# Attention prologue of a fused attention, MoE and ELU-FFN kernel: bias read-outs after the next hidden products, blocks loaded one step earlier, extra products of ones on TensorE

## The chip, the cores and the metric

One core of a Trainium2 chip runs the whole kernel. The metric is the device time of one execution in microseconds (us); the median of three runs of the kernel before is 1201.24 us (1200.07 to 1203.87). The engines are TensorE (PE; its weight loads are PEld), VectorE (DVE), ScalarE (ACT), GpSimd (POOL) and SyncE (SP), which issues the DMAs.

## The reference

Attention over 2 batches, 8 heads, 576 positions and head size 64, with a position bias that a small network makes; its output goes through an MoE and an ELU feed-forward layer. Only the attention is touched.

```python
scores = scale * np.matmul(q, k.transpose(0, 1, 3, 2))
psi_rel = np.log1p(np.abs(rel))                       # 576 x 576
psi_i = np.log1p(np.maximum(pos[:, None], 1.0))
x = (psi_rel / psi_i)[..., None]
h = np.maximum(x @ w1 + b1, 0.0)                      # 32 hidden values
bias = h @ w2                                         # 8 heads
scores = scores + bias.transpose(2, 0, 1)[None, :, :, :]
attn = softmax(scores)
out = np.matmul(attn, v)
```

## The kernel before

**Steps.** The 16 pairs of head pair and batch are "blocks". A step is one tile of up to 128 query rows of one block: scores on TensorE (`emit_qk`, letter Q, tile `sc`, 8 matmuls), bias added and the row minimum taken on DVE (R and S, tile `et`), exponentials on ACT (E and F), and one step later transposes (T, U, V), products with the values (a, tile `av`) and evacuation (X). The first four steps are the 64-row tile of blocks 0 to 3, so each of them needs a block of its own.

**Blocks.** `load_qk(i)` asks SP for block i in four DMAs of 288 KB, into slot i mod 3 of a ring; `prep(i)` splits it into high and low parts in six DVE operations (two casts, two for `qs`, two for `kl`), one per letter p of the prologue, three per p of the first steps. `LQ` and `PS` say at which step blocks 2 and 3 are loaded and at which step each `prep` is queued.

**Bias.** The bias is made in 36 groups of 16 rows, over the prologue and the first fourteen steps. A group has three stages. Letter H (`bias_hh`, `bias_h`): four hidden tiles `ht` of 304 to 576 columns, each put on ACT or DVE by `pick`, which adds up estimated loads of both engines. Letter P or M (`bias_p`, `bias_mm`): the products `bps` on TensorE, four column tiles of 32. Letter O (`bias_o`, `bias_out`): one or two read-outs `o` by ACT or DVE, again by `pick`, and a store to the scratch `scr` in HBM. A step's bias tile `bt` is loaded from `scr` (B, and L through `bias_loads`) once its groups are stored. At most two groups of `ht` may wait for their product (`len(hq) < 2`), and `ht` lies in two pairs of buffers: the tiles of group k take those of group k-2, which the product of group k-2 reads. From step 0 on the products of a group of up to 512 columns lie in one PSUM bank (`psC[1]`), so a product waits for the read-out of the product before it; a longer group takes a bank of `psB` as well.

**Order.** The order on every engine is the order in which these letters are emitted: `PRO` for the prologue, `ORD_S` for steps 0 to 2 (three groups a step), `ORD_A` while groups are left (two a step), `ORD_B` after. Each engine works through its own queue in that order, SP through its DMAs. In the prologue read-outs of the first groups go through `psA`, which the scores use later. Eight products of ones (`WARM`) open the kernel on TensorE while the first DMAs run.

After the bias is done a step holds scores, transposes and value products only; then come the MoE and the feed-forward layers, over 80% of the time.

Of the kernel before, what the change touches and what calls it, by code (L numbers as in the profile page):

```python
# [32 lines left out]
QB = [5, 4]  # L33
AB = 2
BD = 1
PRO = "HHPOH0PpOHpPOHPOkkBHppPkkppOQHmO"
LQ = [100, 101]
LS = [5, 9, 13, 21]
LV = [0, 1, 2, 3, 19, 20, 28, 32]
ACC = [2.6, 3.1]  # L40
WARM = 8
PS = [[1, 0], [2, 1], [3, 2], [4, 13], [5, 16], [6, 20], [7, 26]]
ORD_S = "RXTSMOHUapaMOHEaaNpFaLMOVQH"
ORD_A = "RXTSMOHUapaEaaNpFaLMOVQH"
ORD_B = "RTSNUXaafLEafaappFVQ"
TOFF = [0, 128, 256, 384, 512]
TROW = [128, 128, 128, 128, 64]
# [173 lines left out]
def attention_moe_elu_ffn_kernel(  # L221
# [14 lines left out]
    act, dve, pe, pool, sp = nc.scalar, nc.vector, nc.tensor, nc.gpsimd, nc.sync  # L236
# [12 lines left out]
    def psum(name, bufs, shape):  # L249
        p = ctx.enter_context(tc.tile_pool(name=name, bufs=bufs, space=bass.MemoryType.PSUM))  # L250
        return lambda nm: p.tile(shape, F32, tag=name, name=nm)
# [3 lines left out]
    psC = [psum("psC", 1, [128, 512]), psum("psD", 1, [128, 512])]  # L255
# [4 lines left out]
    ones = cp.tile([128, 128], F32, name="ones")  # L260
# [856 lines left out]
    def attention(fill):  # L1117
# [21 lines left out]
        def load_qk(i):  # L1139
            hp, b = blocks[i]  # L1140
            loaded[i] = []
            for src, rt in ((qt, ring[0]), (kt, ring[1])):
                r = rt[:, i % 3]
                for o in (0, 64):
                    sp.dma_start(out=r[o:o + 64], in_=src[b, hp])
                    yield
                loaded[i].append(r)

        def load_now(i):
            for _ in load_qk(i):  # L1150
                pass
# [7 lines left out]
        prep_q = []  # L1159
# [3 lines left out]
        def prep(i):  # L1163
            qs = qkp.tile([128, 2, S], F32R, tag="qs", name="qs")
            kh = qkp.tile([128, 2, S], F32R, tag="kh", name="kh")
            kl = klp.tile([128, 2, S], F32R, tag="kl", name="kl")
            prepped[blocks[i]] = qs, kh, kl
            qr, kr = loaded.pop(i)
            rem = dve if i < 4 else pool
            for dst, src in ((qs, qr), (kh, kr)):  # L1170
                dve.tensor_copy(dst, src)
                load["d"] += 0.73
                yield
            for h in range(2):
                o = slice(64 - 64 * h, 128 - 64 * h)
                rem.tensor_tensor(out=qs[o, h], in0=qr[o, h], in1=qs.bitcast(F32)[o, h], op=ALU.subtract)
                yield
            for h in range(2):
                rem.tensor_tensor(out=kl[:, h], in0=kr[:, h], in1=kh.bitcast(F32)[:, h], op=ALU.subtract)
                if rem is dve:  # L1180
                    load["d"] += 1.5
                yield
# [17 lines left out]
        def emit_qk(s):  # L1200
            hp, b, t = steps[s]
            qs, kh, kl = prepped[hp, b]
            r = TROW[t]
            etile[s] = (
                ep.tile([128, 2 * S], F32, tag="e", name="et"),
                tp.tile([128, 2], F32, tag="nmx", name="nmx"),
                tp.tile([128, 2], F32, tag="sm", name="sm"),
            )
            sc = [psA("sc") for _ in range(2)]
            qc = slice(TOFF[t], TOFF[t] + r)  # L1210
            for h in range(2):
                for w, last in ((kh, False), (kl, True)):
                    for x in range(2):
                        kc = slice(HALF * x, HALF * x + HALF)
                        pe.matmul(sc[h][0:r, x, 0:HALF], qs[:, h, qc], w[:, h, kc], start=not last, stop=last)  # L1215
            for h in range(2):
                scs[s, h] = sc[h]
# [40 lines left out]
        def emit_tr(s, h):  # L1258
            r = TROW[steps[s][2]]
            et = etile[s][0]  # L1260
            if h == 0:
                aT[s] = atp.tile([128, 9, 128], F32, tag="aT", name="aT")
            p = psB("tr")
            for j in range(4):
                c0 = 640 * h + 128 * j
                pe.transpose(p[:, 128 * j:128 * j + r], et[0:r, c0:c0 + 128], ident[0:r, 0:r])  # L1266
            src = p.rearrange("p (j q) -> p j q", j=4)[:, :, 0:r]
            dst = aT[s][:, 4 * h:4 * h + 4, 0:r]
            if h == 0:
                act.activation(out=dst, in_=src, func=ACTF.Copy)  # L1270
            else:
                dve.tensor_copy(dst, src)

        def emit_trl(s):
            r = TROW[steps[s][2]]
            et = etile.pop(s)[0]
            p = psB("trl")
            pe.transpose(p[:, 0:r], et[0:r, 512:640], ident[0:r, 0:r])  # L1278
            act.activation(out=aT[s][:, 8, 0:r], in_=p[:, 0:r], func=ACTF.Copy)
# [51 lines left out]
        def run_step(s):  # L1331
            d = s - LAG
            cur, tr = s < NS, 0 <= d < NS
            for x in ORD_S if s < 3 else ORD_A if no[0] < GRP else ORD_B:
                if x == "T" and tr:
                    emit_tr(d, 0)
                elif x == "U" and tr:
                    emit_tr(d, 1)
                elif x == "V" and tr:
                    emit_trl(d)  # L1340
                elif x == "Q" and s + 1 < NS:
                    emit_qk(s + 1)
                elif x in "RS" and cur:
                    emit_ttr(s, "RS".index(x))
                elif x in "EF" and cur:
                    emit_exp(s, "EF".index(x))
                elif x == "N" and 1 <= s <= NS:
                    emit_norm(s - 1)
                elif x == "X":
                    x_evac()  # L1350
                elif x == "a":
                    av(1)
                elif x == "M":
                    bias_p()
                elif x == "O":
                    bias_o()
                elif x == "H":
                    bias_hh()
                elif x == "p":
                    for _ in range(3 if s < 4 else 1):  # L1360
                        prep_next()
                    do_bg(1)
                elif x == "L":
                    bias_loads(s)
                elif x == "f":
                    fill_pe(s)
            if tr:
                av_q.extend(av_pieces(d))

        U = up.tile([128, S], F32, name="U")  # L1370
        bpsi = csb[:, C_PSI:C_PSI + NM]
        dve.memset(ones, 1.0)
        wp = psC[0]("warm")
        for _ in range(WARM):
            pe.matmul(wp[:, 0:128], ones, ones, start=True, stop=True)
        sp.dma_start(out=csb, in_=cst)
        sp.dma_start(out=U, in_=lext)
        load_now(0)
        dve.tensor_scalar(bpsi, bpsi, csb[:, C_B1:C_B1 + 1], None, ALU.mult)
        dve.tensor_scalar(U, U, csb[:, C_W1:C_W1 + 1], None, ALU.mult)  # L1380

# [8 lines left out]
        def bias_h(g):  # L1390
# [3 lines left out]
            for c in range(4):  # L1394
# [4 lines left out]
                if pick(0.187 + n / 1200, 0.129 + n / 1920) == "a":  # L1399
                    act.activation(out=h[:, 0:n], in_=U[:, 0:n], func=ACTF.Relu, bias=bpsi[:, m:m + 1])  # L1400
                else:
                    dve.tensor_scalar(h[:, 0:n], U[:, 0:n], bpsi[:, m:m + 1], 0.0, ALU.add, ALU.max)
                ht.append(h)
# [59 lines left out]
        def bias_hh():  # L1463
            if nh[0] < GRP and len(hq) < 2:
                bias_h(gorder[nh[0]])
                nh[0] += 1
# [13 lines left out]
                load_bias(nk[0])  # L1480
                nk[0] += 1

        ld = [load_qk(1)]
        for x in PRO:
            if x == "H":
                bias_hh()
            elif x == "P":
                bias_p(True)
            elif x == "m":
                bias_p()  # L1490
            elif x == "O":
                bias_o()
            elif x == "0":
                prep_q.append(prep(0))
            elif x == "p":
                prep_next()
            elif x == "k":
                next(ld[0], None)
            elif x == "B":
                load_bias(nk[0])  # L1500
                nk[0] += 1
            elif x == "Q":
                emit_qk(0)
        next(ld[0], None)
        for s in range(NS + LAG):
            if 100 + s in LQ:
                load_now(2 + LQ.index(100 + s))
            for i, s0 in enumerate(LS):
# [4 lines left out]
            if s in LV:  # L1513
                load_v(LV.index(s))
            for i, s0 in PS:
                if s == s0:
# [15 lines left out]
            if s == 15:  # L1532
                w = csb[:, C_WG:C_WG + 4 * E].rearrange("p (k e) -> p k e", k=4)
# [86 lines left out]
```

## Time and profile before

| | |
|---|---|
| median of 3 runs | 1201.24 us |
| profiled execution | 1202.67 us, span 1200.8 us |
| busy share PE, PEld, DVE, ACT, POOL | 97%, 83%, 76%, 53%, 6% |
| chain that ended last | PE 93%, ACT 2%, DVE 2%, DMA 1%, issue 1% |
| stretch of the span that the change touches | about the first 115 us |

The span runs from the first to the last instruction of the program. The profiled execution has 1.87 us around its span, and lies 1.43 us over the median. The busy shares are averages over stages with different limits, so the stage of the change is read by itself, in windows and in order of time.

### The profile page before, as it was taken

What the parts mean: (1) busy time and instruction counts of PE and PEld (TensorE: products, weight loads), DVE (VectorE), ACT (ScalarE), POOL (GpSimd) and SP (SyncE); (2) the same over time, 40 slices, a digit from 0 to 9 for tenths busy, and PEclk for the clock granted to TensorE, in tenths of its full rate; (3) what the DMA queues carried; (4) which work ended last, traced back from release to release, by engine and by line L of the source; (5) the groups of instructions that cost most, each with busy time, mean ns of one, the idle gap of its engine ahead of it and who ended that gap; (6) DMA issues with size and microseconds to landing.
All of it is one profiled execution on the core that took longest, in us unless ns stands there. A gap on an engine that the chain in (4) does not pass through costs nothing.

```text
span 1200.8 us, 19646 instructions
## 1 busy us (share of the span) xinstructions
PE 1167.2 (97%) x7432; PEld 996.8 (83%) x7432; DVE 910.5 (76%) x1936; ACT 632.7 (53%) x1428; POOL 67.9 (6%) x91
## 2 busy tenths in 40 slices
PE   6899999899999999999999999999999988999998
PEld 3466988788888888888888888888888876788887
DVE  6688888755687878778778788787776468788875
ACT  6898678554333344444443444444434346777763
POOL 0101643000000000000000000000000001000000
PEclk8999999999999999999999999999999999999999
DMA  7676641111112133333242323332311101111102
GB/s 207 212 227 213 184 141 48 36 53 53 36 36 97 62 106 89 104 90 94 74 132 64 104 90 104 99 96 78 115 45 53 53 3 35 53 53 36 36 1 79
DMA packets 36285, 104.78 MB, mean 87 GB/s; under 512 B 4064, under 2 KB 4192, under 8 KB 36192
## 3 DMA queue, kind: packets, MB, share of 16 engines
q1 hardware_dynamic: 36192, 103.54, 28.3%
q8 instruction: 58, 0.95, 0.3%
q14 instruction: 35, 0.29, 0.1%
HBM read 81.88 MB, written 21.64 MB: 86 GB/s over the span
## 4 chain that ended last, share of the span: by engine, by line
PE 93%; ACT 2%; DVE 2%; DMA 1%; issue 1%; POOL 0%; SPq 0%; DVEq 0%; ACTq 0%; POOLq 0%
PE y L724 41%; PE m L537 38%; PE sc L1215 3%; PE bps L1418 3%; PE av L1297 3%; PE tr L1266 3%; PE av L1307 1%; PE av L1294 1%; PE trl L1278 0%; PE lg L880 0%; ACT ht L1400 0%; DMA bt<-scr 0%; ACT et L1240 0%; ACT o L1450 0%; DVE c L569 0%
## 5 line engine op out<-in xcount | busy, mean ns | idle before, releaser
L537 PE MATMUL m<-oh,w1h 128*128 128x256 f32 (+1 forms) x1120 | 335.3, 299 | 3.9 <-DVE c L569 1.4
L537 PE MATMUL m<-oh,w1l 128*128 128x256 f32 (+1 forms) x1120 | 329.7, 294 | 3.8 <-ACT u L550 1.6
L537 PE MATMUL m<-ol,w1h 128*128 128x256 f32 (+1 forms) x1120 | 329.5, 294 | 2.8 <-DVE c L569 1.3
L724 PE MATMUL y<-w2h,hh 128*128 128x512 f32 x720 | 284.5, 395 | 2.9 <-ACT hh L644 1.5
L724 PE MATMUL y<-w2h,hl 128*128 128x512 f32 x720 | 283.4, 394 | 0.0
L724 PE MATMUL y<-w2l,hh 128*128 128x512 f32 x720 | 282.6, 392 | 0.8 <-DVE w2l L437 0.8
L537 PEld LDWEIGHTS m<-oh,w1h 128*128 128x128 f32 x1120 | 210.0, 188 | 47.4 <-ACT u L550 13.3
L537 PEld LDWEIGHTS m<-ol,w1h 128*128 128x128 f32 x1120 | 210.4, 188 | 22.6 <-DVE c L569 1.9
L537 PEld LDWEIGHTS m<-oh,w1l 128*128 128x128 f32 x1120 | 210.3, 188 | 5.6 <-ACT u L550 2.3
L724 PEld LDWEIGHTS y<-w2h,hh 128*128 128x128 f32 x720 | 135.1, 188 | 18.8 <-ACT hh L644 2.3
L724 PEld LDWEIGHTS y<-w2h,hl 128*128 128x128 f32 x720 | 135.1, 188 | 17.8
L550 ACT ACTIVATE p<-m 128x256 f32<-128x256 f32 (+1 forms) x160 | 65.8, 411 | 157.3 <-PE m L537 153.2
L724 PEld LDWEIGHTS y<-w2l,hh 128*128 128x128 f32 x720 | 135.2, 188 | 16.2 <-DVE w2l L437 1.4
L550 ACT ACTIVATE u<-m 128x256 f32<-128x256 f32 (+1 forms) x160 | 65.9, 412 | 131.8 <-PE m L537 128.5
L600 ACT ACTIVATE hh<-c 128x512 fp32r<-128x512 f32 (+3 forms) x128 | 72.1, 563 | 109.7 <-DVE c L569 109.6
L755 DVE SCALAR_TENSOR_TENSOR acc<-y,P,acc 128x512 f32<-128x512 f32 x126 | 94.5, 750 | 38.5 <-PE y L724 36.6
L603 DVE SCALAR_TENSOR_TENSOR hl<-c,hh 128x512 fp32r<-128x512 f32 (+3 forms) x128 | 77.5, 606 | 20.5 <-ACT hh L600 18.8
L569 DVE TENSOR_TENSOR c<-m,u 128x256 f32<-128x256 f32 (+1 forms) x80 | 36.7, 458 | 72.4 <-PE m L537 70.7
L1225 DVE CUSTOM_DVE_ANT_0 et<-sc,bt 128x576 f32<-128x576 f32 (+1 forms) x80 | 58.1, 751 | 16.0 <-PE sc L1215 14.2
L1240 ACT ACTIVATE et<-et,nmx 128x576 f32<-128x576 f32 (+1 forms) x80 | 61.3, 772 | 0.3 <-DVE nmx L1225 0.3
L430 ACT ACTIVATE w2h<-raw 128x512 fp32r<-128x512 f32 x80 | 48.6, 625 | 23.2 <-PE y L724 12.4
L1418 PE MATMUL bps<-ht,csb 128*32 128x512 f32 (+17 forms) x352 | 48.8, 520 | 9.9 <-ACT ht L1400 5.7
(138 smaller groups left out, 1566.7 us busy)
## 6 DMA issues: line engine op xcount, KB each, us to landing
raw<-w1p SPq DMA_DIRECT2D x32, 512.0 KB, 3.8
raw<-w2p SPq DMA_DIRECT2D x32, 512.0 KB, 3.6
scr<-o SPq DMA_DIRECT2D x36, 295.5 KB, 2.5
bt<-scr SPq DMA_DIRECT2D x16, 576.0 KB, 4.2
cw<-w1d SPq DMA_DIRECT2D x16, 512.0 KB, 4.4
wsc<-ca SPq DMA_DIRECT2D x32, 256.0 KB, 4.5
cw<-w2d SPq DMA_DIRECT2D x16, 512.0 KB, 4.5
raw<-wsc SPq DMA_DIRECT2D x16, 512.0 KB, 3.6
```

Of the source, the lines that this page charges most:

```text
L430: act.activation(out=dst(bh.get()), in_=src(), func=ACTF.Copy)
L537: lambda e, w=w, o=o, j=j, k=k: pe.matmul(x["ap"](bank), w.get()[:, ai, j, :], o.get()[:, bi, j, :], start=(k == 0 and i in (1, 2, 5)), st ...
L550: lambda e: act.activation(out=b.get()[:, 0:N], in_=x["ap"](bank), func=ACTF.Copy),
L569: lambda e: eng[e].tensor_tensor(out=blk(b.get()[:, half * N:half * N + N], rev), in0=ap(p), in1=ap(q), op=ALU.add),
L600: op([("A", cA(w))], lambda e: act.activation(out=hh(), in_=ap(), func=ACTF.Relu), r=sk, w=wh, after=gate_)
L603: lambda e: dve.scalar_tensor_tensor(out=bl.get()[:, d], in0=ap(), scalar=0.0, in1=hhf(), op0=ALU.max, op1=ALU.subtract),
L724: lambda e, a=a, w=w, f=f, i=i, y=y, c=c: pe.matmul(y.get(), a.get()[:, c], w.get(), start=(f == 0 and i == 0), stop=(f == 3 and i == 2)),
L755: lambda e: dve.scalar_tensor_tensor(out=a.get(), in0=y.get(), scalar=P[0][:, n, e_:e_ + 1], in1=a.get(), op0=ALU.mult, op1=ALU.add),
L1215: pe.matmul(sc[h][0:r, x, 0:HALF], qs[:, h, qc], w[:, h, kc], start=not last, stop=last)
L1225: dve.tensor_tensor_reduce(out=e.rearrange("p (x j) -> p x j", x=2), in0=sc[0:r, :, 0:HALF], in1=biast[hp, t][0:r, h].rearrange("p (x j) - ...
L1240: act.activation(out=e, in_=e, func=ACTF.Exp, scale=-1.0, bias=nmx[0:r, h:h + 1], accum_out=sm[0:r, h:h + 1])
L1418: pe.matmul(p[32 * c:32 * c + 32, d0 - lo:d1 - lo], csb[:, C_W2:C_W2 + 32], ht[c][:, d0:d1], start=True, stop=True, tile_position=(0, 32 * c),
```

## The change

The prologue makes seven groups instead of six, with nine instead of seven groups of hidden tiles begun, and two casts of block 1. Within a step each O moves behind the H that followed it (MOH becomes MHO; at the end of the step MOVQH becomes MHOVQ). Block 1 is loaded right behind block 0, block 2 in the place of block 1, block 3 at step 0 instead of step 1; `prep(1)` starts in the prologue, `prep(2)` and `prep(3)` a step earlier. The new letter w puts four products of ones on TensorE: three times in the prologue and twice in step 0.

```diff
-PRO = "HHPOH0PpOHpPOHPOkkBHppPkkppOQHmO"
-LQ = [100, 101]
+PRO = "HHPOH0PpOHpPOHPOkkBHppPwkkHppOQmHOwm1pHpOw"
+LQ = [0, 100]
-PS = [[1, 0], [2, 1], [3, 2], [4, 13], [5, 16], [6, 20], [7, 26]]
-ORD_S = "RXTSMOHUapaMOHEaaNpFaLMOVQH"
-ORD_A = "RXTSMOHUapaEaaNpFaLMOVQH"
+PS = [[2, 0], [3, 1], [4, 13], [5, 16], [6, 20], [7, 26]]
+ORD_S = "RXTSMHOwUapaMHOwEaaNpFaLMHOVQ"
+ORD_A = "RXTSMHOUapaEaaNpFaLMHOVQ"
...
+                elif x == "w" and s == 0:
+                    warm(4)
...
+        def warm(k):
+            wp = psC[0]("warm")
+            for _ in range(k):
+                pe.matmul(wp[:, 0:128], ones, ones, start=True, stop=True)
+
...
         load_now(0)
+        load_now(1)
...
-        ld = [load_qk(1)]
+        ld = [load_qk(2)]
...
-            elif x == "0":
-                prep_q.append(prep(0))
+            elif x in "01":
+                prep_q.append(prep(int(x)))
+            elif x == "w":
+                warm(4)
```

## Rows read from the trace of the kernel before

**Rows 1.** Windows: us, busy us (x instructions) of each engine, granted clock, DMA.

```profile
40.00:50.00 10.00, 9.09 (x60) 3.93 (x60) 7.97 (x17) 8.19 (x19) 1.49 (x1) 1.00 0.50 172
60.00:70.00 10.00, 10.00 (x107) 6.72 (x106) 9.24 (x32) 9.22 (x26) 0.81 (x2) 1.00 0.64 211
130.00:140.00 10.00, 10.00 (x105) 9.18 (x104) 8.90 (x25) 6.90 (x21) 5.46 (x7) 1.00 0.62 220
```

**Rows 2.** Chain that ended last, first 200 us: start, us, what.

```profile
17.68 4.60 DMA bt<-scr
...
24.45 2.65 PE bps L1418 x8
...
28.84 2.53 PE bps L1418 x8
31.37 2.11 PE sc L1215 x8
...
59.07 1.26 PE sc L1215 x8
...
108.16 1.06 PE sc L1215 x8
...
113.77 1.05 PE sc L1215 x8
...
117.31 1.07 PE sc L1215 x8
```

**Rows 3.** Windows of 2 us around the stretch at the lower clock, columns as Rows 1.

```profile
22.00:24.00 2.00, 0.00 (x0) 0.00 (x0) 1.70 (x6) 1.50 (x3) 0.00 (x0) 0.96 0.91 234
24.00:26.00 2.00, 1.55 (x7) 0.84 (x11) 2.00 (x5) 0.00 (x0) 0.00 (x0) 0.50 1.10 381
...
34.00:36.00 2.00, 2.00 (x13) 0.69 (x12) 1.42 (x5) 1.16 (x4) 0.00 (x0) 0.98 1.07 308
```

**Rows 4.** Waits, first 150 us: who for whom, us, times, longest.

```profile
ACT o L1450 <- PE bps L1418: 15.4, 19, 3.6
```

**Rows 5.** Waits, first 30 us.

```profile
ACT o L1450 <- PE bps L1418: 7.5, 5, 3.6
```

**Rows 6.** Timeline, one pair of products: start, us, engine, line, operation, shapes [idle before].

```profile
101.01 0.60 PE L1418 MATMUL bps<-ht,csb 128*32 128x464 f32 x4
...
101.42 0.57 PE L1418 MATMUL bps<-ht,csb 128*32 128x464 f32 x4
```

**Rows 7.** Timeline, 15 to 28 us.

```profile
15.29 1.54 DVE L1176 TENSOR_TENSOR qs<-ring,qs 64x576 fp32r<-64x576 f32 x2
...
16.22 2.66 ACT L1400 ACTIVATE ht<-U,csb 128x544 f32<-128x544 f32 x4
16.76 1.41 DVE L1179 TENSOR_TENSOR kl<-ring,kh 128x576 fp32r<-128x576 f32 x2
...
18.62 1.15 PE L1418 MATMUL bps<-ht,csb 128*32 128x512 f32 x16
...
23.82 1.29 DVE L1402 TENSOR_SCALAR ht<-U,csb 128x528 f32<-128x528 f32 x3
```

**Rows 8.** DMA issues, 1.6 to 4.2 us: count, KB each, median us to landing.

```profile
ring<-qt SPq DMA_DIRECT2D x2, 288.0 KB, 4.6
ring<-kt SPq DMA_DIRECT2D x2, 288.0 KB, 5.8
```

**Rows 9.** Timeline, first 6 us, TensorE.

```profile
1.05 3.78 PE L1375 MATMUL warm<-ones 128*128 128x128 f32 x16 [1.05 <-DVE ones L1372]
```

**Rows 10.** Timeline, 35 to 60 us, ACT and DVE.

```profile
35.84 0.91 ACT L1450 ACTIVATE o<-bps,csb 128x496 f32<-128x496 f32 x2 [0.84 <-PE bps L1418]
36.64 0.70 ACT L1400 ACTIVATE ht<-U,csb 128x480 f32<-128x480 f32 x1
38.46 0.91 ACT L1450 ACTIVATE o<-bps,csb 128x480 f32<-128x480 f32 x2 [1.12 <-PE bps L1418]
...
58.91 0.96 DVE L1452 TENSOR_SCALAR o<-bps,csb 128x384 f32<-128x384 f32 x2 [1.49 <-PE bps L1418]
```

More of the change, by code (lines that the diff above doesn't have):

```diff
@@ L1372, in attention @@
         dve.memset(ones, 1.0)
-        wp = psC[0]("warm")
-        for _ in range(WARM):
-            pe.matmul(wp[:, 0:128], ones, ones, start=True, stop=True)
+        warm(WARM)
         sp.dma_start(out=csb, in_=cst)
```

## The prediction, made before the change was run

> **What bounds the kernel now.** I read the windows first. Of 1200.8 us the change touches the first 115. From 60 to 110 us TensorE reads 10.00 busy in 10, but loads weights for only 6.72 of them, while from 130 us, with the bias done, it loads for 9.18 [rows 1]. So a busy TensorE is partly waiting in the bias stage, and ACT, at 9.22, is as near its limit. Before 60 us nothing is full: 9.09, 8.19 and 7.97 of 10 for TensorE, ACT and DVE.
>
> The chain of waits gives the milestones [rows 2]. Step 0's score pass waits for the bias tile (landed at 17.68 + 4.60 = 22.28 us). The scores of step 1 start at 31.37, of step 4 at 59.07, of step 13 at 108.16, of step 14 at 113.77, of step 15 at 117.31. So steps 4 to 12 last (108.16 - 59.07) / 9 = 5.45 us each, step 13, with one group, 5.61, and a step without bias 3.54. TensorE's granted clock is at the lower level (0.50, 1.2 GHz) from just before 24 to about 34 us, after a gap in which it ran nothing (22 to 24 us) [rows 3]; there two products take 2.65 and 2.53 us [rows 2] where a pair of 512 columns and a rest at the higher level takes 1.15 [rows 7].
>
> The wait which the change names is in the table of waits: ACT's read-outs wait 15.4 us in all for their products, 19 times [rows 4], 7.5 us of it before 30 us [rows 5].
>
> **Where the wait goes.** A product ends as one: four records start together, the other four 0.41 us later, all over by 101.99 [rows 6]. So all its `ht` buffers come free at its end, 0.98 us after its start. Before, ACT waits there with the read-out. In the new order the hidden tiles of group k+2 come first, and they take the very buffers which the product of group k reads; so H waits for the same end. Behind it, O stands later by H, and the next product waits for O, because both use one PSUM bank. A slot before, from read-out to read-out: read-out, hidden tile, tail of the product: 38.46 - 35.84 = 2.62 us, with one hidden tile of four on ACT [rows 10]. After, with the same split: hidden tile 0.6 (0.66 of [rows 7], for fewer columns), read-out 0.9, product 1.0, two hand-overs of 0.05 to 0.1 (the product of [rows 6] runs from 101.01 to 101.99): 2.6 to 2.7. The wait changes its owner; the loop keeps its length. Per slot I take nothing.
>
> **The change part by part**, against the profiled execution (1202.67 us, span 1200.8; 1.43 above the median).
>
> A, to the scores of step 1. Each start below is the end of the last input, from the durations of [rows 7], [rows 6] and [rows 10]: hidden tile 0.66 on ACT and 0.43 on DVE, read-out 0.9, product of 16 records 1.15, of 8 about 1.05, prep operation 0.72; engines as `pick` gives them by the code's own sums. Two hidden tiles of group g2 now stand on DVE ahead of the `kl` of block 0: its scores, and the product behind them, slip from 18.62 to 19.5. That product (g1) ends at 20.65; three tiles on ACT to 22.65; read-out to 23.55; product g2 to 24.8; two tiles to 26.1; read-out to 27.0; product g3 to 28.25; one tile and the read-out to 29.8 (DVE's three tiles beside them); product g4 to 30.95. On DVE three prep operations, a hidden tile and the read-out of g4 end at 33.2, so product g5 ends at 34.35. Then the scores of step 1: 34.35 against 31.37, **+3.0**, with one group more done. The clock's return is in it (products at 1.05 to 1.15). The wait for `bt` is covered: DVE comes to the score pass at 26.
>
> In A cost nothing: the products of ones. Unknown at the higher level; eight records take 1.9 us by the first eight products of the kernel (3.78 for 16) [rows 9], and no less than 0.9 if they run at twice that pace. TensorE's gaps of 3.0, 2.2, 1.6 and 2.3 us (20.65 to 23.65 and so on) hold either, but for 0.3 us at most. Block 1 asked early: four DMAs, issued on an SP that has nothing else until the first store at 9.6; loads of 288 KB land some 1.25 us apart (issue to landing 4.6 for the first pair, 5.8 for the second, issued 1.25 later) [rows 8], so block 1 lands by about 14.6 and the first stores behind it come late by up to 2 us. That moves `bt` by at most the same, to 24.3, with 1.7 us of cover. Block 2 takes block 1's places on SP, block 3 waits for nothing at step 0 (slot 0 was read by 19.1) and is wanted after 40 us.
>
> B, steps 1 to 3: the rest of the low stretch, 31.37 to 34. Scores 1.26 instead of 2.11 (-0.85) [rows 2], and half of the other 0.5 us: **-1.1**. The casts moved forward lie on a DVE that isn't full; nothing.
>
> C, steps 4 to 12. Of the 72 hidden tiles of the last 18 groups `pick` puts 33 on ACT instead of 21, and of their read-outs 10 instead of 3 on DVE. ACT: 12 x 0.6 - 7 x 0.91 = +0.8; DVE: 7 x 0.96 - 12 x 0.4 = +1.9 [rows 7, 10]. Bounds: TensorE's own work is 3.54 + 2 x 0.85 (0.98 scaled to a mean of 400 columns) = 5.24 a step, so 9 x 0.21 = -1.9 at best; at worst the four more slots with three hidden tiles on ACT cost 2 x 0.6 each, +4.8. Read-outs on DVE are what TensorE's bank then waits for, so I take DVE's **+1.9**.
>
> The Trainium skill, Perfetto Trace Analysis, "Identifying the Most-Contended Engine", holds that the busy share of matmuls is a poor measure for TensorE and that the share of weight loads is a better one. Read by the 10.00, TensorE would be full, C nothing and the sum -0.2; read by the rule (6.72 against 9.18 [rows 1]) it has room, and the loop of ACT and DVE decides. The trace bears the rule out so far; the other reading is rival 4.
>
> D: step 13 loses its group: 3.54 for 5.61, **-2.07**.
>
> Sum: 3.0 - 1.1 + 1.9 - 2.07 = +1.7 us: span 1202.5, and 1201.24 + 1.7 = **1203.0** for the median. After step 14 all is as before: loads, prep of blocks 4 to 7 and weights hang on step numbers. A measurement of this kernel can tell about 0.3%, 3.6 us, from no change.
>
> **Rivals.**
> 1. The clock falls again, and the kernel is slower. In the new order a product runs in one piece of 1.0 us instead of stretched over its hidden tiles, so between 37 and 48 us TensorE does less than the 9.09 of [rows 1], with no products of ones there. A low stretch as long as that of before, 10 us, holds four products in the loop at about 1.0 more each: +4.0, 1207.0. It decides from two such products on (1.7 + 2.0 > 3.6). Against it: before, the clock stays at 1.00 through 40 to 50 us. [...] Chance 0.20.
> 2. The wait is really gone, and the kernel is faster: H finds free buffers, ACT never waits for a product after 30 us: -(15.4 - 7.5) = -7.9 in place of C, 1203.0 - 1.9 - 7.9 = 1193.2. Against it: two pairs of buffers and `len(hq) < 2`. Chance 0.13.
> 3. The products of ones don't hold the clock, and it falls at 24 us as before: products g3 and g4 1.1 longer, B gone: +3.3, 1206.3. Chance 0.10.
> 4. TensorE is the bound from 60 us on, C is nothing: 1203.0 - 1.9 = 1201.1. Chance 0.16.
>
> **How the numbers follow.** The forecast, 1203.0, has 0.41. C's bounds alone span 1199.2 to 1205.9; with rivals 1, 3 and 4, and half a run's spread, the range is 1198.8 to 1208.3; it leaves out rival 2 and a little more. Slower by over 0.3% (above 1204.8): rivals 1 and 3 and a tenth of the forecast, 0.34. Faster (below 1197.6): rival 2 and 0.01 of the forecast, 0.14. Between them 0.52: no change that can be told.
>
> **What would show it.** The wait of ACT's read-outs gone from the table of waits, and one about as large of `ht` on ACT and DVE for `bps` in its place; TensorE's wait for `o` grown. Clock 1.00 from 24 to 34 us. Scores of step 1 near 34, of step 4 near 61, of step 14 near 115.5. The prediction is wrong if `ht` doesn't wait for `bps`, if the clock falls anywhere before 60 us, or if steps 4 to 12 come nearer 5.2 than 5.6 us.

## The result, and the profile after

The changed kernel takes 1209.67 us (median of 4, 1209.01 to 1210.27) against 1200.99 us of the kernel before beside it: ratio 1.0068 [1.005, 1.0086], slower by 6 to 10 us. The forecast was 1203.0 us with a range to 1208.3. The profiled execution took 1209.01 us, span 1207.0, 6.2 us over the span of before; by the medians the distance is 8.7 us, since the profiled execution of before lies 1.7 us over its median and that of after 0.7 under.

The first score product of each step, after, from the timeline of TensorE (start, duration, engine, line, operation, shapes):

```profile
34.38 0.48 PE L1215 MATMUL sc<-kh,qs 128*64 128x288 f32 x2
...
65.54 0.54 PE L1215 MATMUL sc<-kh,qs 128*128 128x288 f32 x2
...
117.24 0.50 PE L1215 MATMUL sc<-kh,qs 128*128 128x288 f32 x2
...
120.78 0.51 PE L1215 MATMUL sc<-kh,qs 128*128 128x288 f32 x2
```

These are steps 1, 4, 13 and 14. The same record of before stands at 31.30, 59.00, 107.92 and 113.53 (the chain of [rows 2] enters these passes 0.07 to 0.24 us later). So the stages of the prediction measure:

| stage | predicted | measured |
|---|---|---|
| A, to the scores of step 1 | +3.0 | 34.38 - 31.30 = +3.08 |
| B, steps 1 to 3 | -1.1 | 31.16 - 27.70 = +3.46 |
| C, steps 4 to 12 | +1.9 | 51.70 - 48.92 = +2.78 |
| D, step 13 | -2.07 | 3.54 - 5.61 = -2.07 |
| at step 14 | +1.7 | +7.25 |

At step 20 the distance is still 7.27; about 1 us of it is gone by the end of the span, and where it goes stays open. The miss is B: 4.56 us of the 5.5 that part forecast and measurement at step 14.

The windows of after (us, busy us of PE, PEld, DVE, ACT, POOL, granted clock, DMA share, GB/s); the first, second and last answer to [rows 1]:

```profile
40.00:50.00 10.00, 6.58 (x34) 2.75 (x37) 7.99 (x18) 8.38 (x19) 2.17 (x1) 0.59 0.24 90
60.00:70.00 10.00, 8.81 (x92) 5.35 (x95) 6.38 (x22) 7.53 (x20) 0.39 (x1) 0.91 0.37 128
70.00:110.00 40.00, 37.86 (x368) 24.97 (x365) 34.38 (x102) 36.02 (x88) 2.79 (x7) 1.00 0.69 218
130.00:140.00 10.00, 10.00 (x104) 9.12 (x103) 8.90 (x25) 7.17 (x21) 7.39 (x8) 1.00 0.27 77
```

The kernel before, from 70 to 110 us:

```profile
70.00:110.00 40.00, 40.00 (x374) 26.52 (x377) 34.12 (x101) 37.07 (x94) 3.00 (x7) 1.00 0.70 219
```

From 40 to 50 us TensorE is busy for 6.58 where it was 9.09, at a granted clock of 0.59 where it was 1.00. The records of the clock give the lower level (1.2 GHz) for 24.3 to 27.7, 38.0 to 48.2 and 55.1 to 61.9 us; before, once, for 23.8 to 34.1 [rows 3]. What TensorE did just before each fall, and inside the long one:

```profile
22.00:24.00 2.00, 0.88 (x9) 0.29 (x12) 0.00 (x0) 1.06 (x3) 0.00 (x0) 1.00 1.02 218
36.00:38.00 2.00, 0.28 (x5) 0.16 (x8) 0.62 (x2) 1.98 (x5) 0.00 (x0) 1.00 0.66 192
52.00:55.00 3.00, 1.61 (x21) 0.72 (x21) 2.46 (x6) 1.95 (x5) 0.00 (x0) 1.00 0.43 169
38.00:48.00 10.00, 7.39 (x36) 2.67 (x29) 7.29 (x15) 6.91 (x14) 2.17 (x1) 0.50 0.35 124
```

The waits of the first 150 us (who for whom: us, times, longest):

```profile
DVE ht L1408 <- PE bps L1424: 14.3, 15, 2.2
PEld bps L1424 <- ACT o L1456: 13.3, 14, 2.0
ACT ht L1406 <- PE bps L1424: 12.0, 14, 1.9
PE bps L1424 <- ACT o L1456: 10.7, 11, 1.8
...
ACT o L1456 <- PE bps L1424: 1.5, 3, 0.9
```

The wait of [rows 4], 15.4 us of ACT's read-outs, is down to 1.5, and 26.3 us of hidden tiles waiting for the same products (14.3 on DVE, 12.0 on ACT) stand in its place, with TensorE waiting for the read-outs behind them. One and a half slots of the new loop, at the higher clock:

```profile
48.73 0.88 ACT L1456 ACTIVATE o<-bps,csb 128x448 f32<-128x448 f32 x2
49.66 0.93 PE L1424 MATMUL bps<-ht,csb 128*32 128x432 f32 x8 [0.80 <-ACT o L1456]
50.69 1.67 ACT L1406 ACTIVATE ht<-U,csb 128x400 f32<-128x400 f32 x3 [0.71 <-PE bps L1424]
50.76 0.43 DVE L1408 TENSOR_SCALAR ht<-U,csb 128x400 f32<-128x400 f32 x1 [1.50 <-PE bps L1424]
52.26 0.88 ACT L1456 ACTIVATE o<-bps,csb 128x432 f32<-128x432 f32 x2
53.19 0.91 PE L1424 MATMUL bps<-ht,csb 128*32 128x416 f32 x8 [1.58 <-ACT o L1456]
54.19 1.12 ACT L1406 ACTIVATE ht<-U,csb 128x384 f32<-128x384 f32 x2 [1.05 <-PE bps L1424]
55.22 0.88 ACT L1456 ACTIVATE o<-bps,csb 128x416 f32<-128x416 f32 x2
```

Read-out, product, hidden tiles, read-out: each starts within 0.1 us of the end of the one before it, and none lies beside another. From product to product it takes 53.19 - 49.66 = 3.53 us.

### The profile page after: what moved, and what is told of

It is laid out like the page before. It is cut to its first block, busy times and chain, and to the rows that moved or that the text cites. A ratio compares the mean times of both kernels' runs of the same rounds, so it can differ in the third digit from the quotient of the medians.

```text
span 1207.0 us, 19757 instructions
## 1 busy us (share of the span) xinstructions
PE 1166.6 (97%) x7472; PEld 999.7 (83%) x7472; DVE 912.2 (76%) x1937; ACT 634.1 (53%) x1427; POOL 67.2 (6%) x91
## 4 chain that ended last, share of the span: by engine, by line
PE 90%; ACT 3%; DVE 2%; issue 1%; POOL 0%; DMA 0%; SPq 0%; ACTq 0%; DVEq 0%; POOLq 0%
PE y L724 41%; PE m L537 38%; PE sc L1215 3%; PE av L1297 2%; PE tr L1266 2%; PE bps L1424 2%; ACT ht L1406 1%; PE av L1307 1%; ACT o L1456 1%; PE av L1294 1%; ACT et L1240 0%; PE lg L880 0%; DVE ht L1408 0%; DMA ring<-qt 0%; PE trl L1278 0%
## 5 line engine op out<-in xcount | busy, mean ns | idle before, releaser
L537 PEld LDWEIGHTS m<-ol,w1h 128*128 128x128 f32 x1120 | 210.3, 188 | 22.8 <-DVE c L569 1.9
L1225 DVE CUSTOM_DVE_ANT_0 et<-sc,bt 128x576 f32<-128x576 f32 (+1 forms) x80 | 57.9, 750 | 10.2 <-PE sc L1215 10.0
L1424 PE MATMUL bps<-ht,csb 128*32 128x512 f32 (+17 forms) x352 | 41.9, 552 | 17.0 <-ACT o L1456 10.7
```

What stands on the lines that cost most here:

```text
L537: lambda e, w=w, o=o, j=j, k=k: pe.matmul(x["ap"](bank), w.get()[:, ai, j, :], o.get()[:, bi, j, :], start=(k == 0 and i in (1, 2, 5)), st ...
L1225: dve.tensor_tensor_reduce(out=e.rearrange("p (x j) -> p x j", x=2), in0=sc[0:r, :, 0:HALF], in1=biast[hp, t][0:r, h].rearrange("p (x j) - ...
L1424: pe.matmul(p[32 * c:32 * c + 32, d0 - lo:d1 - lo], csb[:, C_W2:C_W2 + 32], ht[c][:, d0:d1], start=True, stop=True, tile_position=(0, 32 * c),
```

## The experiments

Twelve kernels. Two questions: is it the clock, as the windows suggest, or the order of the loop; and if the order, what in it. The readings of all of them, from the same records as above (us; "clock" is the stretch at the lower level before 100 us; the ratio is to the kernel before on the same chip, whose medians were 1203.05 to 1203.12 beside the experiments and 1200.99 beside after, so that across rows the ratios compare better than the times):

| kernel | step 1 | steps 1-3 | steps 6-12 | step 14 | clock | time, ratio |
|---|---|---|---|---|---|---|
| before | 31.30 | 27.70 | 38.97 | 113.53 | 23.8-34.1 | |
| after | 34.38 | 31.16 | 41.78 | 120.78 | 24.3-27.7, 38.0-48.2, 55.1-61.9 | 1209.67, 1.0068 |
| e1_order_back | 31.77 | 24.71 | 38.45 | 108.01 | 37.3-44.1 | 1199.01, 0.9959 |
| e2_no_warm | 36.53 | 30.98 | 41.76 | 122.72 | 18.2-38.7, 42.1-62.6 | 1213.17, 1.0077 |
| e3_warm_steps | 34.04 | 28.91 | 41.77 | 118.17 | 17.9-21.3 | 1206.78, 1.0034 |
| e4_third_ht | 30.87 | 25.03 | 39.55 | 108.61 | 29.6-33.0, 39.8-50.1 | 1197.87, 0.9952 |
| e5_warm_only | 28.56 | 27.94 | 38.97 | 111.02 | none | 1202.01, 0.9992 |
| e6_loads_only | 31.63 | 27.71 | 38.97 | 113.86 | 23.7-34.0 | 1204.65, 1.0014 |
| e7_two_ahead | 29.27 | 28.86 | 38.10 | 116.84 | 23.4-33.6, 37.0-43.9, 50.7-71.2 | 1197.09, 0.9973 |
| e8_order_back_warm | 32.27 | 29.30 | 38.44 | 113.09 | 19.4-22.8, 36.4-39.8 | 1201.19, 0.9990 |
| e9_two_ahead_warm | 29.69 | 26.35 | 38.09 | 109.19 | 7.8-11.2, 41.9-48.8 | 1194.44, 0.9939 |
| e10_order_alone | 29.41 | 25.37 | 38.88 | 109.75 | 22.4-32.6, 39.5-42.9 | 1199.96, 0.9972 |
| e11_order_alone_warm | 29.19 | 26.35 | 38.87 | 110.48 | 24.3-27.7, 34.5-41.4, 48.2-51.6 | 1198.60, 0.9973 |
| e12_change_one_ahead | 29.87 | 27.39 | 39.03 | 115.06 | 46.6-70.5 | 1201.05, 0.9983 |

Six profiles have a later stretch at the lower level too, of 3.4 or 6.8 us, near 205 to 226 us (e1, e2, e9, e10) or 1015 to 1024 us (e5, e6, e10); before and after have none but in the last 3 us of their spans, as all have. The ratio, with its interval, isn't the quotient of the two medians: for e7, whose times fall into two groups, that quotient would be 0.9950.

**e1: the old order of letters in the changed kernel.**

```diff
-ORD_S = "RXTSMHOwUapaMHOwEaaNpFaLMHOVQ"
-ORD_A = "RXTSMHOUapaEaaNpFaLMHOVQ"
+ORD_S = "RXTSMOHwUapaMOHwEaaNpFaLMOVQH"
+ORD_A = "RXTSMOHUapaEaaNpFaLMOVQH"
```

> The changed kernel with read-outs ahead of the hidden tiles again in the steps (MOH); prologue, loads and products of ones as in the change. Theory 'clock and loop': the wait only changed its owner, and what costs is TensorE's lower clock in steps 1 to 3 (4.6 us) and the prologue (3.1 us); products still run in one piece, two groups being ahead, so the clock falls again and the time stays at 1207 to 1210 us. Rival 'order': the read-out behind the hidden tiles itself lengthens the slots; then steps 1 to 12 take back their 6 to 7 us and the time is 1202 to 1204 us.

1199.01 us, 0.9959 [0.9941, 0.9977]: below both ranges, and faster than the kernel before. Step 14 comes 12.77 us earlier than after, though the lower clock is there from 37.3 to 44.1 us. The clock as the main cause falls; in this kernel it is the order.

```profile
PEld bps L1424 <- ACT o L1456: 11.0, 9, 2.6
PE bps L1424 <- ACT o L1456: 8.2, 8, 1.9
ACT o L1456 <- PE bps L1424: 6.2, 11, 1.3
DVE ht L1408 <- PE bps L1424: 4.8, 9, 1.8
```

The hidden tiles' wait is 4.8 us instead of 26.3, and the read-outs' 6.2 instead of the 15.4 of [rows 4]: with the old order and two groups ahead both waits are small.

**e2: the change without its five groups of products of ones** (the letters w taken out of the prologue, none in step 0).

> The changed kernel without its five letters w (the eight products of ones at the very start stay). Theory 'clock and loop': the products of ones are what held the clock for all but 3.4 us of the stretch from 24 to 38 us; without them it falls there as before, the scores of step 1 start 2 us or more later (36.5 or later instead of 34.4) and the time is 1211 to 1214 us. Rival 'no use': the clock's course doesn't depend on them, or the five stand in TensorE's way; 1207 to 1210 us.

1213.17 us, 1.0077 [1.006, 1.0094]; the lower clock takes 41 us of the first 63, and the scores of step 1 come 2.15 us later than after. So by the profiles the ones of the change are worth some 2 us where they stand; the two ratios, 1.0077 and 1.0068, don't tell that from nothing.

**e3: more products of ones, in steps 1 to 3 of the change.**

```diff
-ORD_S = "RXTSMHOwUapaMHOwEaaNpFaLMHOVQ"
-ORD_A = "RXTSMHOUapaEaaNpFaLMHOVQ"
+ORD_S = "RXTzSMHOwUapaMHOwEaaNpFaLMHOVQ"
+ORD_A = "RXTzSMHOwUapaEaaNpFaLMHOVQ"
...
-                elif x == "w" and s == 0:
-                    warm(4)
+                elif x == "w" and s < 4:
+                    warm(4, s > 0)
+                elif x == "z" and 0 < s < 4:
+                    warm(4, True)
...
-            wp = psC[0]("warm")
+            wp = psA("warm")[:, 0] if late else psC[0]("warm")
...
```

> The changed kernel with four products of ones more at each of nine or so places in steps 1 to 3 (behind the first transposes and behind the read-out letters), so that TensorE has work where the clock fell at 38 and at 55 us. Theory 'clock and loop': granted clock 1.00 from 38 to 62 us, products there 1.0 instead of 1.7 us, scores of step 4 near 61 instead of 65.5, time 1204 to 1206 us. Rival 'order': the clock comes back but products aren't what the slots wait for; scores of step 4 stay past 64, time 1208 to 1211 us.

1206.78 us, 1.0034 [1.0021, 1.0048], and the scores of step 4 at 34.04 + 28.91 = 62.95: between what theory and rival wanted. The window of 38 to 48 us is now at the higher level:

```profile
38.00:48.00 10.00, 7.99 (x69) 5.13 (x65) 8.37 (x18) 8.66 (x19) 2.17 (x1) 1.00 0.37 125
```

Steps 1 to 3 take 28.91 us instead of 31.16, so the held clock gives back 2.25 us there, less whatever the ones cost. Steps 6 to 12 stay at 41.77 for 41.78: the clock has no part in those.

**e4: the change with three sets of hidden buffers** in the memory that was there.

```diff
...
+        hbuf = [wgt.tile([128, 3, S], F32, tag=t, name="ht") for t in ("w1l", "w1l", "w1h", "w1h")]
...
-                if c % 2 == 0:
-                    h2 = wgt.tile([128, 2, S], F32, tag="w1h" if c else "w1l", name="ht")
-                h = h2[:, c % 2]
+                j = 4 * (hbn[0] % 3) + c
+                h = hbuf[j // 3][:, j % 3]
...
```

> The changed kernel with three sets of hidden-tile buffers instead of two, in the same memory, so that the tiles of group k+2 don't take those which the product of group k reads. Theory 'clock and loop': the waits of ACT and DVE hidden tiles for products (12.0 and 14.3 us in the first 150) nearly vanish, each slot loses up to 1 us of ACT's standing, and the time falls by 4 to 9 us, to 1201 to 1206. If the hidden tiles' wait isn't what holds the loop, the wait goes to the read-outs or to TensorE's bank and the time stays within 2 us of 1209.7.

1197.87 us, 0.9952 [0.9937, 0.9967], 3 us below the theory's range; step 14 at 108.61, and no wait of `ht` for `bps` is left in the table. The order of letters is that of the change, and so is the split over the engines (30 hidden tiles on ACT and 16 read-outs on DVE in steps 4 to 12, as in after). Only the buffers differ, so the shared buffers are the cause. The Trainium skill, Perfetto Trace Analysis, "Optimization Strategy", says that the same gap repeating for a stretch can mean too little memory for the next tile; the 29 waits of `ht` in after, gone with a third set, agree.

**e5: the kernel before with products of ones only** (w in the prologue behind the fifth product and at its end, and twice in step 0).

> The kernel before, with four of the five groups of products of ones that fit its letters (two in the prologue, two in step 0) and nothing else of the change. If the lower clock from 24 to 34 us costs the kernel before what its products there show against the higher clock (about 1.1 us each for two, and 0.85 us of one score pass) and the ones hold it, the scores of step 1 start about 1 to 2 us before 31.30 and the time is 1 to 2 us under the kernel before. If the gap from 22 to 24 us still lets the clock fall, the ones only stand in the way: 0 to 1.5 us over it, with the granted clock again at 0.50 to 34 us or later.

1202.01 us, 0.9992 [0.9979, 1.0006]. The profile shows the higher level throughout these steps:

```profile
24.00:34.00 10.00, 8.81 (x56) 3.92 (x50) 7.94 (x17) 7.90 (x18) 0.00 (x0) 1.00 1.04 294
```

The scores of step 1 come 2.74 us early, more than the theory's 1 to 2, and step 14 comes 2.51 early; but steps 1 to 3, at the higher clock too, take 27.94 us for 27.70. The median gains only 1 us, and the interval doesn't tell that from none. The profile has a stretch of 3.4 us at the lower clock near 1017 us that the profile of before lacks, which would be 1.7 us of the difference.

**e6: the early loads only.**

> The kernel before, with block 1 asked right behind block 0, block 2 in its place and block 3 at step 0; the casts stay where they were. If the wait for blocks is no part of the matter, as I took it, the step starts stay within 0.5 us of the kernel before (31.3 and 59.0) and the time within 1 us. If the early loads delay the first stores and with them the bias tile past what DVE covers, the scores of step 1 start up to 2 us later and the time is up to 2 us longer. If blocks 1 to 3 came late before, steps 1 to 3 get shorter and the time is 1 us or more shorter.

1204.65 us, 1.0014 [1.0, 1.0027]: steps within 0.35 us of the kernel before, and a median 1.6 us over it, past the 1 us expected. The profile has 3.4 us at the lower clock near 1020 us, which would be 1.7 us. In the steps the loads show no part in either direction.

**e7: the kernel before with one more H at the end of the prologue**, so that two groups are begun ahead: one letter.

```diff
-PRO = "HHPOH0PpOHpPOHPOkkBHppPkkppOQHmO"
+PRO = "HHPOH0PpOHpPOHPOkkBHppPkkppOQHmOH"
```

> The kernel before, with one more group of hidden tiles at the end of the prologue, so that two groups are always begun ahead of a product; no new order, no loads, no ones. Theory (two groups ahead under the order product, read-out, hidden tiles is what gains, because a read-out has the hidden tiles of another group beside it): most of the 5.5 us that the change with the old order is ahead of the kernel before at step 14, so 3 to 5 us under the kernel before, with step 14 near 109 to 110.5 us instead of 113.5. Rival (the extra whole group in the prologue, the loads and the ones gain it): within 1 us of the kernel before.

1197.09 us, 0.9973 [0.9946, 0.9999], with six times from 1193.76 to 1197.72 at a mean clock of 0.989 to 0.996 and four from 1204.02 to 1205.18 at 0.983 to 0.985. The profile is of the longer kind:

```profile
50.00:60.00 10.00, 9.77 (x58) 5.81 (x58) 5.87 (x17) 7.52 (x21) 0.76 (x2) 0.53 0.37 134
60.00:70.00 10.00, 10.00 (x62) 6.17 (x65) 5.36 (x19) 5.06 (x14) 0.40 (x1) 0.50 0.51 159
```

With 58 and 62 matmuls, where [rows 1] has 107 in the second of these windows, and the lower clock, step 14 is at 116.84 where the theory wanted 109 to 110.5: missed in the profile. The time was to be 3 to 5 us under the kernel before: by the ratio it is 3.2, by the medians 6.0, and the interval ends just under 1. In steps 6 to 12, once the clock is back, it gains 0.87 us.

**e8: the old order, and ones in steps 1 to 3** (e1 and e3 together).

> The change with the old order (product, read-out, hidden tiles), and more products of ones in steps 1 to 3, as in the run that had them with the new order. If the stretch at the lower clock from 37.3 to 44.1 us still costs the old order something (some three products at about 0.8 us more), the clock holds and the time is 1 to 2.5 us under the change with the old order alone (1199.01). If its products lie beside ACT's and DVE's work there, so that the lower clock costs nothing, or the ones themselves stand ahead of products, it is the same or up to 2 us longer.

1201.19 us, 0.9990 [0.9972, 1.0008], 2 us slower than e1 by the medians: steps 1 to 3 take 29.30 us instead of 24.71, with less of the lower clock. These ones use the bank of the scores, and wait there for DVE:

```profile
PEld warm L1377 <- DVE nmx L1225: 2.6, 2, 1.3
PE warm L1377 <- DVE nmx L1225: 2.3, 2, 1.2
```

That they stand in the way is shown; these rows don't account for all of the 4.6 us. In e3 the same ones wait for DVE too (0.8 us), so its 2.25 us are a lower end of what the clock took.

**e9: two groups ahead and e5's ones, in the kernel before.**

```diff
-PRO = "HHPOH0PpOHpPOHPOkkBHppPkkppOQHmO"
+PRO = "HHPOH0PpOHpPOHPOkkBHppPwkkppOQHmOwH"
-ORD_S = "RXTSMOHUapaMOHEaaNpFaLMOVQH"
+ORD_S = "RXTSMOHwUapaMOHwEaaNpFaLMOVQH"
```

> The kernel before with one more group of hidden tiles at the end of the prologue and the four groups of products of ones that held the clock in the kernel before. The run with the extra group alone fell into two groups of times, near 1195 and near 1204.5 us; its profile, of the longer kind (1205.18), shows the lower clock in 23 to 34, 37 to 44 and 51 to 71 us, and its mean clock is lower in all runs of that kind. Theory (the slots are shorter with two groups ahead, and only the clock takes it back): with the clock held in the first stretch the times gather near the shorter kind or below it, 1192 to 1197 us, step 14 near 104 to 108 us. Rival (the shorter slots themselves leave TensorE too little to do, whatever went before): lower clock again between 37 and 71 us and a time of 1200 to 1205 us in the profiled execution.

1194.44 us, 0.9939 [0.9919, 0.9959], the fastest of all: 7.3 us (5 to 10) under the kernel before. Six of its nine times are 1192.75 to 1194.53 at a mean clock of 0.996 to 0.998; three, the profiled one among them, are 1197.85 to 1200.22 at 0.992 to 0.993, with the clock down from 41.9 to 48.8 us in the profile, and again for 6.8 us from 205.8. So the theory's range holds the median, and the rival's the profiled execution; step 14, at 109.19, comes later than the theory's 104 to 108.

**e10: the new order of letters alone**, in the kernel before, with one group ahead.

```diff
-ORD_S = "RXTSMOHUapaMOHEaaNpFaLMOVQH"
-ORD_A = "RXTSMOHUapaEaaNpFaLMOVQH"
+ORD_S = "RXTSMHOUapaMHOEaaNpFaLMHOVQ"
+ORD_A = "RXTSMHOUapaEaaNpFaLMHOVQ"
```

> The kernel before with the new order of letters in the steps (product, hidden tiles, read-out) and nothing else: only one group is begun ahead, so the hidden tiles that stand behind product k are those of group k+1, whose buffers the product of group k-1 has left long ago. Theory (the new order costs time only because, with two groups ahead, its hidden tiles need the buffers of the product in front of them): nothing waits there, the slot is a product beside hidden tiles, then a read-out, 2.1 to 2.3 us; step 14 comes 3 to 7 us before the 113.53 us of the kernel before, the wait of ht for bps stays under 3 us in the first 150, and the time is 1196 to 1201 us unless the clock falls once more. Rival (the new order is slow by itself, since every read-out and the product behind it come a hidden tile later): step 14 at 116 to 121 us and 1204 to 1210 us.

1199.96 us, 0.9972 [0.9957, 0.9987]; step 14 at 109.75, 3.78 us early. No wait of `ht` for `bps` stands in its table. The new order isn't slow by itself; it gains.

**e11: the same with e5's ones.**

> The new order of letters in the steps with one group ahead, as in the run of the order alone, and the four groups of products of ones. Theory: as the order alone with the first stretch of lower clock gone, 1 to 3 us under it: step 14 near 104 to 108 us, 1193 to 1199 us. Rival: the order is slow by itself and the ones change nothing of that, 1203 us or more.

1198.60 us, 0.9973 [0.9953, 0.9993], in the theory's range; but the clock isn't held (24.3 to 27.7, 34.5 to 41.4 and 48.2 to 51.6 us), step 14 is at 110.48, later than in e10, and the ratio is that of e10. The ones gave nothing here.

**e12: the change, less one letter.**

```diff
-PRO = "HHPOH0PpOHpPOHPOkkBHppPwkkHppOQmHOwm1pHpOw"
+PRO = "HHPOH0PpOHpPOHPOkkBHppPwkkHppOQmHOwm1ppOw"
```

> The change whole, but for one letter: the last group of hidden tiles in the prologue is left out, so one group instead of two is begun ahead, and from step 0 on the hidden tiles behind a product take buffers that are free. Theory (in the change the two parts, two groups ahead and hidden tiles ahead of the read-out, undo each other): the waits of ht for bps fall from 26.3 us on both engines to under 5, step 14 comes 8 to 13 us before the 120.78 of the change, and the time is 1197 to 1202 us. Rival (the new order is slow whatever the number of groups ahead): within 3 us of the change, 1206 to 1211 us.

1201.05 us, 0.9983 [0.9967, 1.0]. Step 14 comes 5.72 us before that of after, less than the 8 to 13 expected, since the clock is at the lower level for 24 us (46.6 to 70.5; its steps 4 to 12 take 54.25 us, those of after 51.70); but steps 6 to 12 need 39.03 instead of 41.78, and the scores of step 1 come at 29.87 instead of 34.38. The waits of `ht` for `bps` are gone. What is left is TensorE for the read-out:

```profile
PEld bps L1424 <- ACT o L1456: 8.4, 7, 2.0
PE bps L1424 <- ACT o L1456: 6.5, 7, 1.8
```

and a slot of it, at the higher clock:

```profile
41.49 1.11 DVE L1408 TENSOR_SCALAR ht<-U,csb 128x416 f32<-128x416 f32 x3
41.71 0.93 PE L1424 MATMUL bps<-ht,csb 128*32 128x432 f32 x8 [0.98 <-ACT o L1456]
41.91 0.65 ACT L1406 ACTIVATE ht<-U,csb 128x416 f32<-128x416 f32 x1
42.71 0.90 ACT L1456 ACTIVATE o<-bps,csb 128x432 f32<-128x432 f32 x2
43.50 1.66 ACT L1406 ACTIVATE ht<-U,csb 128x400 f32<-128x400 f32 x3
43.66 0.91 PE L1424 MATMUL bps<-ht,csb 128*32 128x416 f32 x8
```

DVE's hidden tiles start 0.2 us before the product and ACT's 0.2 us after it, instead of behind its end (they have the 416 columns of the next product; those of the slot of after have the 400 of the one after it). The next product comes 1.95 us after this one: product and read-out, and the hidden tiles beside them (one on ACT here, three in the slot of after).

**What follows.** The hidden tiles can lie beside a product in two ways. With two groups ahead, product k+1 needs only the read-out of k, and the tiles of k+2, which stand behind that read-out, run beside it (e1, e7, e9). In e1, behind the read-out of the product of 448 columns, the tiles of 416 run beside the product of 432:

```profile
43.39 0.89 ACT L1456 ACTIVATE o<-bps,csb 128x448 f32<-128x448 f32 x2
44.27 2.24 ACT L1406 ACTIVATE ht<-U,csb 128x416 f32<-128x416 f32 x4
44.70 0.93 PE L1424 MATMUL bps<-ht,csb 128*32 128x432 f32 x8
```

With one group ahead and the tiles in front of the read-out, those of k+1 run beside product k (e10, e12). The change does both, and then the tiles in front of the read-out are those of k+2, whose two sets of buffers end with the group that product k reads. Each half alone is faster than the kernel before (e10, and e7 by an interval that ends just under 1); the two together put product, tiles and read-out in a row. A third set of buffers takes that away as well (e4). The row has one more link, the single PSUM bank for which TensorE waits until the read-out is done; no run loosened it.

## Why the prediction was wrong, point by point

- **Where the wait goes: right.** H waits for the product that O waited for, O and the next product come behind it: 15.4 us of one wait became 26.3 of the other. "Per slot I take nothing" holds about, where both kernels keep the higher clock: in steps 1 to 3, 8 groups, 28.91 us (e3) for 27.94 (e5), 0.12 us a slot with e3's ones in it; in steps 6 to 12, 14 groups, (41.78 - 38.97) / 14 = 0.20.
- **A, +3.0: right in size** (+3.08), worked out as the row of product, tiles and read-outs that the timeline shows. What I called the price of one more group was that row: e12 makes the same seven groups in the prologue and begins its scores at 29.87, e4 with all nine at 30.87 (e12 without, e4 with 1.3 us of the lower clock ahead of them). The clock wasn't held all through A: 24.3 to 27.7 us.
- **B, -1.1: this step failed**; it measured +3.46. It took the clock as back for good. Rival 1, 0.20 in the prediction, is what happened, and twice: from 38.0 and from 55.1 us, after stretches in which TensorE ran 0.28 us of 2 and 1.61 of 3; a fall before 60 us was one of the prediction's own signs of being wrong. I had the argument for it (a product in one piece leaves TensorE less to do than the 9.09 of [rows 1]) and let the clock of the kernel before, 1.00 through 40 to 50, speak against it; but that row belongs to products stretched over their hidden tiles. Of the 4.56 us by which B missed, e3 gives back 2.25 or more: that much the two stretches, 10.2 + 6.8 = 17.0 us, cost at least. Rival 1's price, +4.0 for one of 10 us, is neither confirmed nor refuted by such a lower end. Another 1.34 is a gain that wasn't there: e5 holds the clock in the kernel before, and its steps 1 to 3 take 0.24 us more than before, not 1.1 less; what the clock gave back there lies ahead of step 1. The last 0.97 is what e3 (28.91) takes over e5 (27.94), the new loop with e3's ones, which no run separates.
- **C, +1.9: inside its bounds (+2.78), for a wrong reason.** I put it down to the split, more tiles on ACT and read-outs on DVE. e10 has such a split in steps 4 to 12 (31 and 15, before 21 and 5) and takes 49.02 us for 48.92; e4 has that of after and takes 49.18. It is the wait for the buffers: in steps 6 to 12 e4 lets 2.23 us of 2.81 go with the split as it was, and e12 2.75, with fewer tiles on ACT and read-outs on DVE (20 and 8, after 25 and 14). What the split adds to the row while the tiles wait, no run separates.
- **D, -2.07: right** to the hundredth.
- **Rival 2** (the wait really gone) named what keeps it from coming, two pairs of buffers and `len(hq) < 2`. With a third set (e4), or with one group ahead instead of two (e12), the hidden tiles don't wait for products; ACT's read-outs still do, for 4.5 us in e4 and 2.1 in e12, and the times are 1197.87 and 1201.05 us where the rival had 1193.2.
- **Rival 3** fell but for 3.4 us: e2 shows the clock down from 18.2 to 38.7 us without the ones.
- **Rival 4** (TensorE the bound) fell for the change: 37.86 us busy in 70 to 110 and 2.8 us longer. For the kernel before it is nearer the truth: there TensorE is busy for all 40.00 us, and in e1 too. The Trainium skill, Perfetto Trace Analysis, "Identifying the Most-Contended Engine", would read room out of 6.72 of 10 for weight loads; yet five orders of the loop (e1, e7, e9, e10, e12) all need 38.09 to 39.03 us for steps 6 to 12, where before needs 38.97. None of them took room of that size, nor came to the 5.24 us a step that the prediction worked out as TensorE's own work (e7, the shortest: 38.09 / 7 = 5.44); whether a sixth order could stays open. Most of what e1, e9, e10 and e12 gain lies ahead of 60 us and, in e1 and e12, in step 13.
- **Free of cost:** the early loads were, by the steps (e6, within 0.35 us). The products of ones cost nothing that shows where the prediction had them, in the prologue (e5 comes to step 1 earlier than the kernel before), though they didn't hold the clock all through it (24.3 to 27.7 us); those that e3 and e8 add in steps 1 to 3 do cost something (e8).

The prediction compared the new loop with the old one, slot for slot, and stopped there. It didn't ask what each half of the change would have done alone, which would have shown the loop that was possible.

## What to carry to other kernels

Before a consumer is moved behind a producer, write down what that producer waits for: look-ahead in the order and look-ahead in the buffers must be counted together, and two ways of hiding the same work may cancel each other. When a long operation gets shorter by being fed at once, see what its engine does in the time that comes free, since the clock may fall there. A stage can measure what was forecast for a reason that isn't so; a run with the reason alone tells.

## What the runs showed of the hardware that I had not expected

Eight records of a bias product of 464 columns took 1.77 us in the stretch at the lower clock (after, timeline); those of 432 columns above took 0.93 behind it:

```profile
41.02 1.77 PE L1424 MATMUL bps<-ht,csb 128*32 128x464 f32 x8 [0.98 <-DVE o L1458]
```

TensorE needn't stand still for the clock to stay low: in e12 it was busy throughout and the clock stayed at 0.50 for over 20 us (windows):

```profile
48.00:58.00 10.00, 10.00 (x60) 5.74 (x57) 5.18 (x16) 5.92 (x17) 0.49 (x2) 0.50 0.54 175
58.00:70.00 12.00, 12.00 (x72) 7.44 (x71) 6.68 (x21) 6.05 (x16) 0.40 (x1) 0.50 0.46 149
```

Nor is the time at the lower level the same in every execution of one program: the times of e7 lie in two groups some 9 us apart, the longer ones with the lower mean clock (0.983 to 0.985, against 0.989 to 0.996). Why the longer stretches last as long as they do stays open.
